# Gated linear attention with a cosine router: token rows made head by head on 64x64 tiles, in y's two PSUM banks, ahead of the scores and one chunk later

## The chip, the cores and the metric

The kernel runs on one core of one Trainium2 chip. The metric is the device time of one execution in microseconds; the time given for a kernel is the median of its runs. A profile is one execution recorded instruction by instruction. In it PE is TensorE's matrix multiply, PEld its weight load, DVE is VectorE, ACT is ScalarE, POOL is GpSimd and SP is SyncE, which issues most of the transfers.

## What is computed

Four batches of eight heads, 768 tokens each, head size 48, all in fp32. A gated linear attention gives `y`; its heads, side by side, are the 384 features of 3072 tokens. A router then picks one of eight experts for every token by the cosine between the token and an expert's embedding, and the expert is a two-layer network.

```python
for t in range(S):
    state = alpha[:, :, t, :, None] * state + np.einsum('bhd,bhe->bhde', k[:, :, t], v[:, :, t])
    y[:, :, t] = np.einsum('bhd,bhde->bhe', q[:, :, t], state)
...
x = y.transpose(0, 2, 1, 3).reshape(B * S, H * D)
xn = x / (np.linalg.norm(x, axis=-1, keepdims=True) + 1e-06)
en = expert_emb / (np.linalg.norm(expert_emb, axis=-1, keepdims=True) + 1e-06)
logits = xn @ en.T / tau
expert_idx = np.argmax(logits, axis=1)
...
for e in range(E):
    h = np.maximum(x[mask] @ w1[e], 0.0)
    out[mask] = gate_w[mask, None] * (h @ w2[e])
```

## The kernel before

The kernel has two phases. The first walks 24 chunks of 128 tokens (six for each batch) and makes the attention output; the second runs the eight experts over their tokens. The change touches only the first.

A head is padded from 48 to 64, so two heads fill 128 partitions. Four such pairs (`NP` = 4) make a chunk. `hh` is the head within a pair, 0 or 1, and it is also the half of the array's rows that the head's 64 features occupy.

The loop over `s` is a software pipeline written by hand. In step `s` TensorE does, in this order: `keys_back(s-1)` (decayed keys turned back, tile `pkb`); `decays(s)` (decay factors, keys and queries turned: tiles `pa`, `pk`, `pq`); `scores(s-1)` (key times query, tiles `sc0` and `sc1`); `mix_states(s-2)` and `mix_chunk(s-2)` (the state's and the chunk's own part of y, tiles `pyx0` and `pyx1`); `update(s-1)` (the new state, tile `pd`); and `rows(s-2)` (tile `px`). After a group of chunks that `GROUPS` names, `choose` (VectorE and GpSimd) picks each token's expert and `place` (TensorE tile `rk`, then VectorE) gives each token its row in the buffer `xs`, sorted by expert; `to_rows` sends the rows there with one indirect DMA per chunk from GpSimd. `in_turn()` pins the order of TensorE's instructions to the order of the calls; `behind(s)` puts small work behind the large VectorE and GpSimd operations of step `s`. The other engines' order is the scheduler's.

The PSUM memory has eight banks of 512 fp32 a partition, and the pools divide them: three for `ps_tr` (everything that is turned, and `px`), two for the scores, two for y (`ps_y`), one for `ps_mm`. A tile of a pool with one buffer is written anew in every step, and the framework inserts the waits: a writer waits for whoever still reads the tile's former content.

In `mix_chunk` the chunk's part of y is made in two halves. Four matmuls write `pyx0` from `sm0`, ScalarE copies `pyx0` to SBUF (`ycols0`, line 615), four matmuls write `pyx1` from `sm1`, and ScalarE copies `pyx1` (`ycols1`). The result is y with features on the partitions and tokens along the free dimension.

`rows` turns that into token rows, and makes the logits in the same pass: it multiplies y, as the stationary operand, by `sel`, which holds two 48-column identities and eight columns of scaled expert embeddings for each pair of heads. One matmul takes all 128 partitions (two heads), gives 64 tokens, and has 2 x 48 + 8 = 104 columns. ScalarE copies the logits (`lg`, line 637) and the rows (`x`, line 638) out of `px`, and VectorE adds up the logits (line 642).

At the end of the walk, steps 24 to 26, the last chunks are finished while the first layer of the first expert runs on the tokens that came early (`first_layer_early`, tile `phe`). The tokens of this early part are fetched by `fetch_early`, the first weights by `weights(0)`, both on SP's queue.

An fp32 matmul of the program stands in the profile as two records[...]; a transpose stands there as one.

Of the kernel before, what the change touches and what calls it, by code (L numbers as in the profile page):

```python
# [9 lines left out]
FP32 = mybir.dt.float32  # L10
# [17 lines left out]
def kernel(  # L28
# [26 lines left out]
    HALF = P // 2  # L55
# [3 lines left out]
    LG, TK, ROW = DM, DM + E, DM + E + 1  # L59
# [6 lines left out]
    S0, EARLY = 16, 2  # L66
# [123 lines left out]
    def mm(*args, **kwargs):  # L190
        last["pe"] = nc.tensor.matmul(*args, **kwargs)  # L191
# [4 lines left out]
    def in_turn():  # L196
        return tc.issue_after(last["pe"].ins) if last else ExitStack()


    with ExitStack() as c1:  # L200
# [40 lines left out]
        a_r, q_r, k_r, v_r = (t.rearrange(chunk_of, p=P) for t in (alpha, q, k, v))  # L241


        sel = keep.tile([P, 2, NP // 2, 2 * D + E], FP32, name="sel")
        group_of = [g for g, (a, b) in enumerate(GROUPS) for _ in range(a, b)]
        x_g = {}

# [5 lines left out]
        def prepare_fills():  # L253
            nc.gpsimd.memset(embp, 0.0)
            nc.gpsimd.memset(sel, 0.0)
            for hh in range(2):
                for q in range(NP // 2):
                    nc.gpsimd.tensor_copy(sel[0:DP, hh, q, 0:D], ident[0:DP, 0:D])
                    nc.gpsimd.tensor_copy(
                        sel[DP:P, hh, q, D : 2 * D], ident[DP:P, DP : DP + D]  # L260
                    )

        def prepare_loads():
            a0 = work.tile([NS, H, DP], FP32, name="a0", bufs=1)
# [36 lines left out]
        def turn_logits():  # L301

            pe = ps_tr.tile([P, 2, NP // 2, E], FP32, tag="tr", name="pe")
            for hh in range(2):
                for q in range(NP // 2):
                    tr(
                        pe[:, hh, q],
                        embp[:, hh, q].rearrange("e j d -> e (j d)"), ident[:E, :E],
                    )
            nc.vector.tensor_copy(sel[:, :, :, 2 * D :], pe)  # L310

        def to_rows(rows, x):
            ins = nc.gpsimd.indirect_dma_start(  # L313
# [269 lines left out]
        NQ = NP // 2  # L583
        YX = NQ * P

        def mix_states(s):
            d = st[s]
            d["pyx"] = pyx = [ps_y.tile([P, 512], FP32, name=f"pyx{hh}") for hh in range(2)]
            dec = d.get("dec")
            if dec is not None:  # L590
                for q in range(NQ):
                    for j in range(2):
                        for i in range(2):
                            hh, p = i, 2 * q + (i + j) % 2
# [22 lines left out]
        def rows(s):  # L617

            yT = st[s]["yT"]
            px = ps_tr.tile([P, 2, NQ, 2 * D + E], FP32, tag="tr", name="px")  # L620
            for hh in range(2):
                for q in range(NQ):

                    for i in range(2):
                        sl = slice(i * HALF, (i + 1) * HALF)
                        mm(
                            px[sl, hh, q], lhsT=yT[hh][:, q, sl], rhs=sel[:, hh, q],
                            start=True, stop=True, skip_group_check=True,
                        )
            g = group_of[s]  # L630
            s0, s1 = GROUPS[g]
            if s == s0:
                x_g[g] = work.tile([P, GMAX, ROW], FP32, name="x", bufs=4)[:, 0 : s1 - s0]
            x = x_g[g][:, s - s0]

            lg = work.tile([P, 2, NQ, E], FP32, name="lg", bufs=1)
            nc.scalar.copy(lg, px[:, :, :, 2 * D :])
            nc.scalar.copy(
                x[:, 0:DM].rearrange("t (q j a d) -> t a q j d", q=NQ, j=2, a=2),
                px[:, :, :, 0 : 2 * D].rearrange("t a q (j d) -> t a q j d", j=2),  # L640
            )
            nc.vector.tensor_reduce(
                x[:, LG : LG + E].unsqueeze(2), lg.rearrange("t a q e -> t e a q"),
                axis=AX.XY, op=ALU.add,
            )

# [28 lines left out]
        send = []  # L675
        placed_at = {}
        for g, (_, s1) in enumerate(GROUPS):
            soon = s1 == S0 or s1 > NS - 3
            placed_at.setdefault(s1 + (2 if soon else 3), []).append(g)
        warm(7)  # L680
        fixed_parts()
        load(0)
# [3 lines left out]
        for s in range(NS + 3):  # L686
            if s + 2 <= NS:
                v_last = load(s + 2)
            if s + 2 == NS:

                with tc.issue_after(v_last.ins):
                    weights(0)
            if 0 <= s - 1 < NS:
                with in_turn():
                    keys_back(s - 1)
            if s < NS:
                decays(s)
            if s == NS:
                with in_turn():
                    turn_early()  # L700
            if s < NS:
                decay_queries(s)
            if 0 <= s - 1 < NS:
                decay_state(s - 1)

                with in_turn(), tc.issue_after(st[s]["a_scan"].ins) if s < NS else ExitStack():
                    scores(s - 1)
            if s == 0:
                with behind(s), in_turn():
                    prepare_first(a0)  # L710
                with behind(s):
                    prepare_logits()
            if NS <= s < NS + 2:
                with in_turn():
                    first_layer_early(2 * (s - NS), 2 * (s - NS) + 1)
            if 0 <= s - 2 < NS:
                with in_turn():
                    mix_states(s - 2)
                with in_turn():
                    mix_chunk(s - 2)  # L720
            if 0 <= s - 1 < NS:

                with in_turn(), tc.issue_after(st[s]["a_scan"].ins) if s < NS else ExitStack():
                    update(s - 1)
            if 0 < s < NS and s % NCH == 0:

                with in_turn():
                    keys_back(s, ps_mm, "mm")
            if NS <= s < NS + 2:
                with in_turn():  # L730
                    first_layer_early(2 * (s - NS) + 1, 2 * (s - NS) + 2)
            if 0 <= s - 2 < NS:
                with in_turn():
                    rows(s - 2)
            if s == 1:
                with in_turn():
                    turn_logits()
            if s == 2:
                with behind(s):
                    routing_constants()  # L740
            if s == 3:
                with behind(s):
                    convert_constants()
            if 4 <= s < 4 + NXG * (NC + 1):
                i, t = divmod(s - 4, NC + 1)
                with behind(s):
                    nc.gpsimd.memset(xg_s[i][:, t], 0.0)
            if s == 3:
                with behind(s):
                    nc.gpsimd.memset(blank, 0.0)  # L750

            for g in placed_at.get(s, ()):
                r = GROUPS[g][1] - 1
                with in_turn():
                    n = place(g, r in (S0 - 1, NS - 1))
                if r == S0 - 1:
                    with behind(s):
                        first_expert(n)

            with behind(s) if s < NS else tc.issue_after(st[NS - 1]["masked"].ins):  # L760
                n_now = len(send) if s >= NS else 0 if s == NS - 1 else 1 + (len(send) > 2)
                for c in send[:n_now]:
                    to_rows(dest[:, c : c + 1], x_g[group_of[c]][:, c - GROUPS[group_of[c]][0]])
                    send.remove(c)
                    if c == S0 - 1:
                        fetch_early()
            if s == NS - 1:
                weights(1)
            r = s - 2
            if 0 <= r < NS:  # L770
                g = group_of[r]
                if r == GROUPS[g][1] - 1:
                    choose(g)
                    with behind(s) if s < NS else ExitStack():
                        nc.gpsimd.tensor_copy(x_g[g][:, :, TK], toks[:, slice(*GROUPS[g])])
            if s > NS:
                with in_turn():
                    first_layer_early(2 * (s - NS) + 2, 2 * (s - NS) + 4)
# [487 lines left out]
```

## Time and profile before

| | us |
|---|---|
| median of 3 runs | 416.75 |
| lowest and highest run | 415.18, 416.89 |
| the profiled execution, device time | 415.06 |
| span of that profile, first to last instruction | 413.3 |
| walk over the chunks, first to last `px` matmul | 18.8 to 150.2 |
| one step of that walk, where no routing falls in it | 5.6 |

The difference of 1.8 us between span and device time lies before the first and after the last instruction. The granted TensorE clock is 0.994 over the span. Busy time is given for each engine, and for TensorE it is modelled, since matmuls overlap: where one group of matmuls begins tells more than how long a single one lasts.

### The profile page before, as it was taken

The page shows a single profiled execution, that of the slowest core. Times are in us where ns is not written, and L with a number is a line of the kernel's source. Part 1 is how long each engine was busy: PE and PEld are TensorE (multiplying, and loading weights), DVE is VectorE, ACT ScalarE, POOL GpSimd, SP SyncE. Part 2 cuts the span into 40 slices and gives each one's busy share as a digit, 9 for nine tenths or more (in the row PEclk, how much of TensorE's full clock was granted, in tenths as well). Part 3 has the DMA queues.
Part 4 walks back from the last instruction along what each step waited for, and adds up shares of the span by engine and source line. Part 5 has one row for each costly group of instructions (what it writes and reads, how often), then busy time and mean ns, then how long its engine had stood idle before and what let it go on. Part 6 is the DMA issues. An engine that isn't in the chain of part 4 may idle for free. (4 is left out here: it accounts for less than half of the span.)

```text
span 413.3 us, 11425 instructions
## 1 busy us (share of the span) xinstructions
PE 403.6 (98%) x4346; PEld 358.6 (87%) x4346; DVE 267.8 (65%) x725; ACT 178.4 (43%) x430; POOL 190.9 (46%) x283
## 2 busy tenths in 40 slices
PE   6999999999999999999999999999999999999994
PEld 6888999899889886879799799799989979979974
DVE  6899788788898334715855845943672694593541
ACT  4555554555455435453523523522451352452410
POOL 7446787777766547308018028024301802702701
PEclk9999999999999999999999999999999999999999
DMA  9999999999998944959009219117303801001001
GB/s 137 160 162 157 159 214 172 199 182 205 194 185 257 387 172 143 293 186 365 6 18 321 92 39 329 56 38 272 121 19 105 302 2 38 22 0 53 3 17 43
DMA packets 119374, 60.20 MB, mean 146 GB/s; under 512 B 102287, under 2 KB 113816, under 8 KB 119312
## 3 DMA queue, kind: packets, MB, share of 16 engines
q1 hardware_dynamic: 115208, 49.14, 51.0%
q0 software_dynamic: 3728, 10.16, 7.1%
q8 instruction: 41, 0.67, 0.8%
q14 instruction: 21, 0.17, 0.1%
q10 hardware_dynamic: 376, 0.05, 0.1%
HBM read 49.69 MB, written 11.45 MB: 148 GB/s over the span
## 5 line engine op out<-in xcount | busy, mean ns | idle before, releaser
L817 POOL DMA_INDIRECT out_dram<-y,sx x25 | 24.4, 977 | 158.1 <-DVE gsh L873 77.6
L999 PE MATMUL pq<-xT,w 128*128 128x192 f32 x280 | 64.5, 328 | 0.6
L922 DVE TENSOR_TENSOR hT<-pq,v 128x192 f32<-128x192 f32 x84 | 30.0, 357 | 32.8 <-PE pq L999 30.8
L999 PEld LDWEIGHTS pq<-xT,w 128*128 128x128 f32 x280 | 47.3, 190 | 2.8 <-DVEq L1165 1.7
L507 POOL TENSOR_TENSOR qs<-qc,a 128x512 f32<-128x512 f32 x24 | 30.6, 1275 | 33.9 <-DVE a L503 23.4
L906 PE MATMUL pyo<-w,hT 128*128 128x384 f32 x128 | 43.3, 492 | 0.0
L906 PEld LDWEIGHTS pyo<-w,hT 128*128 128x128 f32 x128 | 23.7, 190 | 15.3
L999 PE MATMUL pq<-xT_m,w_m 128*128 128x192 f32 x168 | 36.5, 326 | 0.0
L1007 ACT ACTIVATE hT<-hT 128x384 f32<-128x384 f32 (+1 forms) x56 | 24.8, 443 | 23.1 <-DVE hT L922 19.9
L479 DVE TENSOR_TENSOR_SCAN r<-pa,inr 128x511 f32<-128x511 f32 x24 | 29.2, 1216 | 6.3 <-PE pa L194 4.4
L503 DVE TENSOR_TENSOR_SCAN a<-pa,ini 128x512 f32<-128x512 f32 x24 | 29.3, 1223 | 1.1
L1047 PE MATMUL pq<-w_m,hT_m 128*128 128x192 f32 x168 | 29.6, 326 | 0.0
L946 POOL TENSOR_TENSOR w_m<-w 128x384 f32<-128x384 f32 x28 | 27.4, 998 | 3.5 <-DMA out_dram<-y,sx 2.7
L999 PEld LDWEIGHTS pq<-xT_m,w_m 128*128 128x128 f32 x168 | 28.9, 190 | 0.0
L313 POOL DMA_INDIRECT xs<-x,dest x24 | 24.3, 1012 | 9.5 <-issue 4.5
L1007 ACT ACTIVATE hT<-pq 128x192 f32<-128x192 f32 x28 | 9.2, 330 | 43.5 <-PE pq L999 43.5
L1047 PEld LDWEIGHTS pq<-w_m,hT_m 128*128 128x128 f32 x168 | 27.7, 190 | 0.0
L946 POOL TENSOR_TENSOR w_m<-w,w_m 128x384 f32<-128x384 f32 x28 | 27.1, 996 | 0.0
L191 PE MATMUL sc<-qs,kr 64*64 64x128 f32 x768 | 26.5, 276 | 0.0
L191 PE MATMUL pyx<-sm,vt 128*64 128x128 f32 x384 | 26.3, 279 | 0.0
L922 DVE TENSOR_TENSOR v<-pq,v 128x192 f32<-128x192 f32 x56 | 20.0, 356 | 9.1 <-ACT v L1010 4.4
L1054 DVE SCALAR_TENSOR_TENSOR y<-pq,gt,u 128x192 f32<-128x192 f32 x21 | 8.8, 418 | 24.6 <-PE pq L1047 24.6
(199 smaller groups left out, 896.5 us busy)
## 6 DMA issues: line engine op xcount, KB each, us to landing
w<-in_moe_w_dram SPq DMA_DIRECT2D x16, 1536.0 KB, 9.2
kt<-in_k_dram SPq DMA_DIRECT2D x24, 192.0 KB, 4.3
qt<-in_q_dram SPq DMA_DIRECT2D x24, 192.0 KB, 4.5
vt<-in_v_dram SPq DMA_DIRECT2D x24, 192.0 KB, 5.8
xg<-xs SPq DMA_DIRECT2D x22, 196.5 KB, 7.7
at<-in_alpha_dram SPq DMA_DIRECT2D x24, 168.0 KB, 5.0
xg<-xs SPq DMA_DIRECT2D x8, 98.2 KB
at<-in_alpha_dram SPq DMA_DIRECT2D x24, 22.5 KB, 4.2
```

Source lines behind the costliest of these rows:

```text
L191: last["pe"] = nc.tensor.matmul(*args, **kwargs)
L313: ins = nc.gpsimd.indirect_dma_start(out=xs, out_offset=bass.IndirectOffsetOnAxis(ap=rows, axis=0), in_=x, in_offset=None, bounds_check=E ...
L479: nc.vector.tensor_tensor_scan(r[:, L - 2 :: -1], pa[:, L - 1 : 0 : -1], inr[:, L - 2 :: -1], 1.0, ALU.mult, ALU.add,)
L503: d["a_scan"] = by_dve = nc.vector.tensor_tensor_scan(a, pa, ini, 0.0, ALU.mult, ALU.add)
L507: by_pool = nc.gpsimd.tensor_tensor(qs.rearrange("p n t -> p (n t)"), d["qc"], a, ALU.mult)
L817: ins = nc.gpsimd.indirect_dma_start(out=out, out_offset=bass.IndirectOffsetOnAxis(ap=col, axis=0), in_=y, in_offset=None, bounds_check=N - 1,
L906: pe[:] = [nc.tensor.matmul(py, lhsT=hT[:, f], rhs=w2_t[:, f], start=(f == 0), stop=(f == FT - 1),)]
L922: dve[:] = [call(*args)]
L946: nc.gpsimd.tensor_tensor(to[:, f], x[:, f], y[:, f], ALU.subtract)
L999: pe[:] = [nc.tensor.matmul(to, lhsT=left, rhs=right, start=start, stop=stop, skip_group_check=True,)]
L1007: return nc.scalar.activation(h, p, AF.Relu)
L1047: pe[:] = [nc.tensor.matmul(to, lhsT=left[:, f], rhs=right[:, f], start=start and f == 0, stop=stop and f == n - 1, skip_group_check=True,)]
```

## The change

`rows` no longer takes two heads in one matmul. Each head has its own: 64 partitions of y, 64 tokens, and 48 + 8 = 56 columns, on one 64x64 quarter of the array. There are twice as many matmuls, 16 for a chunk in place of 8 (32 records in place of 16). The logits are then eight partial sums for a token instead of four, and ScalarE copies 64 numbers a token rather than 32.

The tile `px` is no longer in `ps_tr`. Both banks of y become one tile of two banks, `pyx`, which `y_banks()` hands out as two halves for `mix_states` and `mix_chunk`, and `rows` takes the same tile anew: heads in the lower half of the rows write its first bank, heads in the upper half its second.

`rows` moves. It stood at the end of the step, for chunk `s-2`; now it stands in front of `scores(s-1)`, for chunk `s-3`. In the last steps it is called twice to catch up: step 24 does chunk 21 in front and chunk 22 behind, step 25 does chunk 23. `choose` follows `rows`, so it comes one step later, and `placed_at` moves the groups: `place` comes a step later for all groups but the last two. The rows of chunks 16 to 19 are placed in step 24 rather than 23, and the sending of those rows follows it.

```diff
-        sel = keep.tile([P, 2, NP // 2, 2 * D + E], FP32, name="sel")
+        sel = keep.tile([P, 2, NP // 2, D + E], FP32, name="sel")
...
+        def y_banks():
+            both = ps_y.tile([P, 2, 512], FP32, name="pyx")
+            return both[:, 0], both[:, 1]
+
         def mix_states(s):
             d = st[s]
-            d["pyx"] = pyx = [ps_y.tile([P, 512], FP32, name=f"pyx{hh}") for hh in range(2)]
+            d["pyx"] = pyx = y_banks()
...
         def rows(s):
 
             yT = st[s]["yT"]
-            px = ps_tr.tile([P, 2, NQ, 2 * D + E], FP32, tag="tr", name="px")
+            both = ps_y.tile([P, 2, 512], FP32, name="pyx")
+            px = both[:, :, 0 : NP * (D + E)].rearrange(
+                "t j (a q c) -> t j a q c", a=2, q=NQ
+            )
             for hh in range(2):
                 for q in range(NQ):
-
                     for i in range(2):
-                        sl = slice(i * HALF, (i + 1) * HALF)
-                        mm(
-                            px[sl, hh, q], lhsT=yT[hh][:, q, sl], rhs=sel[:, hh, q],
-                            start=True, stop=True, skip_group_check=True,
-                        )
+                        to = slice(i * HALF, (i + 1) * HALF)
+                        for j in range(2):
+                            sl = slice(DP * j, DP * j + DP)
+                            mm(
+                                px[to, j, hh, q], lhsT=yT[hh][sl, q, to], rhs=sel[sl, hh, q],
+                                start=True, stop=True, skip_group_check=True,
+                            )
...
-            lg = work.tile([P, 2, NQ, E], FP32, name="lg", bufs=1)
-            nc.scalar.copy(lg, px[:, :, :, 2 * D :])
+            lg = work.tile([P, 2, NP, E], FP32, name="lg", bufs=1)
             nc.scalar.copy(
-                x[:, 0:DM].rearrange("t (q j a d) -> t a q j d", q=NQ, j=2, a=2),
-                px[:, :, :, 0 : 2 * D].rearrange("t a q (j d) -> t a q j d", j=2),
+                lg, both[:, :, 0 : NP * (D + E)].rearrange("t j (c e) -> t j c e", c=NP)[:, :, :, D:]
+            )
+            nc.scalar.copy(
+                x[:, 0:DM].rearrange("t (q j a d) -> t j a q d", q=NQ, j=2, a=2),
+                px[:, :, :, :, 0:D],
             )
...
-            soon = s1 == S0 or s1 > NS - 3
-            placed_at.setdefault(s1 + (2 if soon else 3), []).append(g)
+            late = 2 if s1 > NS - 3 else 3 if s1 == S0 else 4
+            placed_at.setdefault(s1 + late, []).append(g)
+
+        def rows_of(s):
+            if s < NS:
+                return [s - 3] if s >= 3 else []
+            return {NS: [NS - 3, NS - 2], NS + 1: [NS - 1]}.get(s, [])
...
             if s < NS:
                 decay_queries(s)
+            if 3 <= s <= NS:
+                with in_turn():
+                    rows(s - 3)
             if 0 <= s - 1 < NS:
                 decay_state(s - 1)
...
-            if 0 <= s - 2 < NS:
+            if NS <= s < NS + 2:
                 with in_turn():
                     rows(s - 2)
...
-            r = s - 2
-            if 0 <= r < NS:
+            for r in rows_of(s):
                 g = group_of[r]
                 if r == GROUPS[g][1] - 1:
                     choose(g)
```

More of the change, by code (lines that the diff above doesn't have):

```diff
@@ L258, in prepare_fills @@
                     nc.gpsimd.tensor_copy(sel[0:DP, hh, q, 0:D], ident[0:DP, 0:D])
-                    nc.gpsimd.tensor_copy(
-                        sel[DP:P, hh, q, D : 2 * D], ident[DP:P, DP : DP + D]
-                    )
+                    nc.gpsimd.tensor_copy(sel[DP:P, hh, q, 0:D], ident[DP:P, DP : DP + D])
         def prepare_loads():
@@ L309, in turn_logits @@
                     )
-            nc.vector.tensor_copy(sel[:, :, :, 2 * D :], pe)
+            nc.vector.tensor_copy(sel[:, :, :, D:], pe)
         def to_rows(rows, x):
@@ L624, in rows @@
                     for i in range(2):
-                        sl = slice(i * HALF, (i + 1) * HALF)
-                        mm(
-                            px[sl, hh, q], lhsT=yT[hh][:, q, sl], rhs=sel[:, hh, q],
-                            start=True, stop=True, skip_group_check=True,
-                        )
+                        to = slice(i * HALF, (i + 1) * HALF)
[5 more added lines that the diff above has]
+                            )
             g = group_of[s]
@@ L634, in rows @@
             x = x_g[g][:, s - s0]
-            lg = work.tile([P, 2, NQ, E], FP32, name="lg", bufs=1)
-            nc.scalar.copy(lg, px[:, :, :, 2 * D :])
+            lg = work.tile([P, 2, NP, E], FP32, name="lg", bufs=1)
             nc.scalar.copy(
-                x[:, 0:DM].rearrange("t (q j a d) -> t a q j d", q=NQ, j=2, a=2),
-                px[:, :, :, 0 : 2 * D].rearrange("t a q (j d) -> t a q j d", j=2),
+                lg, both[:, :, 0 : NP * (D + E)].rearrange("t j (c e) -> t j c e", c=NP)[:, :, :, D:]
[3 more added lines that the diff above has]
+                px[:, :, :, :, 0:D],
             )
             nc.vector.tensor_reduce(
-                x[:, LG : LG + E].unsqueeze(2), lg.rearrange("t a q e -> t e a q"),
+                x[:, LG : LG + E].unsqueeze(2), lg.rearrange("t j c e -> t e j c"),
                 axis=AX.XY, op=ALU.add,
```

## The prediction, made before the changed kernel ran

> **What bounds the kernel now.** I read the page's busy table first, then the busy time by stage, then the order of time within one step of the walk, then who waited for whom on TensorE.
>
> ```profile
> span 413.3 us, 11425 instructions
> PE 403.6 (98%) x4346; PEld 358.6 (87%) x4346; DVE 267.8 (65%) x725; ACT 178.4 (43%) x430; POOL 190.9 (46%) x283
> ```
>
> ```profile
> 58.22:63.82 5.60, 5.60 (x115) 5.09 (x113) 4.95 (x11) 3.07 (x7) 4.23 (x12) 1.00 1.21 205
> 63.82:69.41 5.59, 5.59 (x114) 5.08 (x113) 4.89 (x9) 3.07 (x7) 3.72 (x6) 1.00 0.84 148
> ```
>
> These are two whole steps (length, then PE, PEld, DVE, ACT, POOL busy, clock, DMA share, GB/s). PE has no gap in either, PEld is busy 91%, VectorE 88%, ScalarE only 55%. The next view, in order of time, shows why PE's figure can be believed here: its groups begin at a fixed pace.
>
> ```profile
> 60.14 1.10 PE L191 MATMUL sc<-qs,kr 64*64 64x128 f32 x32
> 60.30 0.59 ACT L489 COPY qc<-pq 128x512 f32<-128x512 f32 x1 [0.80 <-PE pq L194]
> ...
> 61.06 0.62 PE L191 MATMUL pyx<-qs,dec 64*64 64x128 f32 x16
> ...
> 61.61 1.09 PE L191 MATMUL pyx<-sm,vt 128*64 128x128 f32 x16
> ...
> 62.32 0.81 ACT L615 COPY ycols<-pyx 128x256 f32<-128x256 f32 x2 [0.34 <-PE pyx L191]
> ...
> 62.54 0.64 PE L191 MATMUL pd<-vt,kb 128*64 128x64 f32 x16
> ...
> 63.00 0.89 PE L191 MATMUL px<-sel,ycols 128*64 128x104 f32 x16
> ...
> 63.82 0.66 PE L194 MATMUL pkb<-ident,kr 128*128 128x128 f32 x4
> 63.93 0.18 ACT L637 COPY lg<-px 128x32 f32<-128x32 f32 x1 [0.81 <-PE px L191]
> ...
> 64.02 0.49 ACT L638 COPY x<-px 128x384 f32<-128x384 f32 x1
> ```
>
> Read the starts. 32 records of the scores take 0.92 us from start to start: eight sets of four (four quarters of the array at once), about 0.11 each for 128 columns. pyx<-sm: 16 records in 0.93, eight pairs, again 0.11 to 0.12. pd: eight pairs of 64 columns in 0.46, 0.058 each. px: 0.82. So the walk is bound by TensorE's stream, and what is added to or taken from TensorE there counts in full. The waits of TensorE's weight loads between 10 and 150 us confirm it: ACT's copy of y holds it three times in all.
>
> ```profile
> PEld px L191 <- issue: 0.7, 2, 0.3
> PEld pkb L194 <- issue: 0.5, 3, 0.2
> ...
> PEld px L191 <- ACT ycols L615: 0.5, 3, 0.2
> ```
>
> **What the Trainium skill says.** "TensorEngine Tiling (Array Packing)", Key Properties: changing the tiling mode drains TensorE. The trace agrees: pq to sc takes 0.55 where pk to pq took 0.44, and dec to sm 0.55 where four sets of 0.11 make 0.44, so a switch costs 0.11. "PSUM — Partial Sum Buffer", on collisions: row tiles may not write one bank at the same time, hence two banks for the two heads; nothing in this trace tests that. "TensorE: Matmul & The Clock Gate", on the measured gaps, has a floor of about 25 ns from one matmul's start to the next. The trace's smallest sustained spacing is 0.46/16 = 29 ns, so it cannot settle whether four quarters share that floor. "Perfetto Trace Analysis", Identifying Dependency Chains, advises reading an instruction's own list of semaphores. I did that for the changed program, and it decides this forecast.
>
> **The change part by part**, against the profiled execution's 415.06 us (span 413.3 and 1.8 around it; the median of the runs, 416.75, is 1.7 higher).
>
> 1. The matmuls of rows. Removed: px's 0.82 less one switch of 0.11 = 0.71, eight pairs of 0.089. The switch stays, it now falls between pd and pkb: three switches a step before (pq to sc, dec to sm, px to pkb) and three after. Added: 32 records of 56 columns in eight sets of four. The nearest row is pd, 64 columns on the same 64-wide weight load, at 0.058; by columns alone (0.109 for 128, 0.089 for 104) it would be 0.051. I take 0.055: 0.44. Gain 0.27 a chunk, times 24 = 6.6. Bounds: 0.30 a chunk (7.2), and below nothing: with the skill's floor shared by the quarters 32 x 0.025 = 0.80, a loss of 2.2 in all.
>
> 2. A wait inside y. Before, pyx0 and pyx1 were two tiles; now both banks are one tile. In the changed program the first matmul of the second half (sm1 into the second bank) has, beside its wait for GpSimd's mask, a new wait on ScalarE, and its value is the copy ycols0 of the same chunk. It is there in all 24 chunks. The first half must thus be finished, copied out by ScalarE and signalled before TensorE may write the second bank. From the lines above: the first half starts at 61.61, the second at about 61.61 + 0.49 = 62.10 (half of the 0.93, with the switch at its front); the first copy starts at 62.32 and lasts 0.372 (each of the 48 copies does, in the view of the tile ycols), so it ends at 62.69. Then comes a signal of about 0.05 (px ended at 63.89, lg began at 63.93) and a restart with its weights not loaded ahead, which I price at 0.05 as half a switch. 62.79 less 62.10 = 0.70 a chunk, times 24 = 16.8. Bounds 0.60 and 0.80 (14.4 to 19.2). Behind the waiting matmul stand the rest of the half, pd, and the next step's pkb and pa: everything on TensorE. VectorE gets pa later, but it is 88% busy of a step that gets longer, so nothing else is late because of it.
>
> 3. A wait in front of y. mix_states writes the tile that ScalarE reads for lg and x; the changed program lists that wait on x, at the first dec matmul. Say the rows' matmuls start at 0. Their last starts at 0.50 and ends 0.22 later (pd's mean record, 0.222), 0.72; ScalarE has finished qc at 0.17 + 0.59 = 0.76; lg begins there, and x ends 0.66 to 0.69 after px's end as in the lines above (63.89 to 64.51), so at about 1.43, and is seen at 1.48. The scores cover it until 0.49 + 0.92 = 1.41. Left over: 0.07, and with the restart 0.12, times the 21 chunks with this sequence = 2.5. Bounds 0 and 5 (0.24 each): the cover is the scores alone, and it is short by a hair.
>
> 4. What goes away: the two switches more that pkb's late place brought at the three batch ends where it stood between y and px, 3 x 0.22 = 0.7; and place's wait for GpSimd's sums at 109.2, 0.5 (the group of chunks 14 and 15 now has nearly a whole step between choose and place). 1.2 together, 0.6 to 1.5.
>
> 5. The last steps. The rows of chunks 16 to 19 are now placed in step 24 behind px(22), and the changed program puts their four indirect DMAs on GpSimd in front of the sums that place needs in step 25. With px(22) at 0: dest is there at 1.65, four DMAs of 1.29 (start to start) run from 1.9 to 7.0, three sums 0.25 each to about 7.6. TensorE reaches that rk at 6.3 without part 2 and 7.0 with it: 0.6 of waiting. Bounds 0 and 1.5. Behind it stand twelve phe matmuls and the second layer.
>
> 6. At nothing: ScalarE's 32 more numbers for lg (about 0.03 of the 45% it is idle); the reduction likewise on VectorE; choose's five operations now in front of sm0 on VectorE, about 1.2 late, but the scores' banks are needed only about 2.4 later. SP's loads and the early fetch move by one step at most, and since TensorE gets slower they have more room: the early tokens landed near 128 and are turned at 137.6.
>
> Sum: -6.6 + 16.8 + 2.5 - 1.2 + 0.6 = +12.1. On the profiled execution that is 427.2, on the median 428.8.
>
> **The rivals.**
>
> *The wait inside y does not bite* (the other side: faster). One mechanism: the second bank's first matmul finds the copy done, or ScalarE's read is short enough to lie under work already queued. Its place is the step from sm0 to sm1, its price part 2's 16.8, and it turns to a gain once this wait costs less than 0.20 a chunk (4.7 / 24). For it: the two halves are in different banks and no data passes between them. Against: the wait is in the program, TensorE runs in order, and the copy ended 0.59 after the second half began. Time: 416.75 - 6.6 + 2.5 - 1.2 + 0.6 = 412.1. Chance 0.08.
>
> *The quarters do not run four at once for short matmuls.* Each set of four costs four issue slots, so rows takes 0.80 or more, and everything else is as forecast: 6.6 + 2.2 more, 437.6. For it: 25 ns is a floor on the skill's page, and no row here goes below 29. Against: the scores' sets of four begin in one burst. Chance 0.12.
>
> *Gain and waits cancel* (within 2 us): the wait is half as long and the restart free, about 417. Chance 0.03.
>
> **How the numbers follow.** The forecast has 0.77. Its own range, from the bounds of parts 1 to 5 taken not all at once, is 423 to 434. With 0.12 at 437.6 and 0.11 below, 422 to 437 leaves out the faster cases and the upper part of the second rival, about 0.2. About 0.5%, 2 us, is what a measurement of this kernel tells from no change. Faster 0.08, same 0.03, slower 0.89.
>
> **What would show it.** Right: in the list of waits a row of some 24 waits of PEld pyx on ACT ycols, about 0.6 each; a second, smaller one on ACT x; the step 6.1 to 6.2 instead of 5.59; rows in 0.40 to 0.48 from its start to the scores' start; PE busy with gaps in the walk. Wrong: no such waits (first rival), or rows at 0.8 (second). If the walk is longer but by less, the restart was cheaper than part 2 has it. The experts' phase should keep its length.

## The result, and the profile after

The changed kernel took 438.88 us (median of 4 runs, 437.70 to 440.45) against 416.78 us before (415.18 to 416.89): ratio 1.054, 95% interval 1.050 to 1.058. It is slower, as forecast, but by 22.1 us and not by 12.0, and it lies above the range that was given. The profiled execution has 438.62 us and a span of 436.8, 23.5 more than the span before.

The head of the page and one whole step of the walk by window (length, then PE, PEld, DVE, ACT, POOL busy with instruction counts, clock, DMA share, GB/s):

```profile
span 436.8 us, 12224 instructions
PE 403.5 (92%) x4730; PEld 352.5 (81%) x4730; DVE 273.8 (63%) x725; ACT 179.1 (41%) x430; POOL 190.9 (44%) x283
```

```profile
59.10:65.32 6.22, 5.66 (x141) 4.89 (x136) 4.40 (x7) 3.09 (x8) 4.98 (x7) 1.00 1.09 233
```

PE's busy time is what it was (403.6 before). The span grew, so what came in is idle time: PE filled a whole step before, and now it stands for 0.56 us of it (and again in the step after this one). The view in order of time says where (start, length, engine, line, operation, and in brackets the idle time ahead of it and what ended it):

```profile
64.86 0.69 PE L191 MATMUL pyx<-sel,ycols 64*64 64x56 f32 x32
...
65.37 1.06 PE L191 MATMUL sc<-qs,kr 64*64 64x128 f32 x32
...
65.73 0.49 ACT L646 COPY x<-pyx 128x384 f32<-128x384 f32 x1
...
66.27 0.67 PE L191 MATMUL pyx<-qs,dec 64*64 64x128 f32 x16
...
66.87 0.66 PE L191 MATMUL pyx<-sm,vt 128*64 128x128 f32 x8
...
67.57 0.37 ACT L617 COPY ycols<-pyx 128x256 f32<-128x256 f32 x1 [0.41 <-PE pyx L191]
...
68.09 0.66 PE L191 MATMUL pyx<-sm,vt 128*64 128x128 f32 x8 [0.56 <-ACT ycols L617]
...
68.55 0.66 PE L191 MATMUL pd<-vt,kb 128*64 128x64 f32 x16
...
69.14 0.66 PE L194 MATMUL pkb<-ident,kr 128*128 128x128 f32 x4
```

Read the starts on PE. rows to scores 0.51; scores to dec 0.90 (0.92 before); dec to the first half 0.60 (0.55); first half to pd 1.68 (0.93), of which first half to second half is 1.22; pd to pkb 0.59, where pd, px and the switch took 1.28. So a step gains 1.28 - 0.59 - 0.51 = 0.18 by the new matmuls, loses 0.75 inside y and 0.03 around dec: +0.60, and the step went from 5.59 to 6.20.

24 times 0.60 are 14.4 us of 23.5. Most of the other 9 stands in the list of PE's waits (total us, times, longest). Its first row is the wait inside y; the row counts PE's idle time alone, 0.56 each, while by the starts, which don't depend on the modelled ends, it costs 0.75 a chunk.

```profile
PE pyx L191 <- ACT ycols L617: 13.5, 24, 0.6
PE pq L1015 <- issue: 2.1, 2, 1.7
PE rk L191 <- DVE state L555: 1.9, 2, 1.3
...
PE rk L191 <- ACT kb L522: 1.3, 2, 0.7
PE sc L191 <- issue: 0.9, 1, 0.9
...
PE rk L191 <- DVE state L553: 0.5, 1, 0.5
```

Two things are new here. rk, the small matmul of place, waits five times, 3.7 us in all, where before only one wait of 0.5 stood. And PE stands three times, 3.0 us in all, in the middle of a row of like matmuls for nothing that the profile shows ("issue"): once in the scores of step 24, twice in the experts' phase. Last, the end: from the issue of the last scatter to the end of the span it is 6.27 us (430.58 to 436.85) against 4.08 (409.19 to 413.27), 2.2 more.

The longest of rk's waits, in order of time:

```profile
105.63 0.66 PE L191 MATMUL pd<-vt,kb 128*64 128x64 f32 x16
...
106.40 0.17 DVE L337 TENSOR_TENSOR chosen<-win,best 128x16 f32<-128x16 f32 x1
106.50 0.68 DVE L572 TENSOR_TENSOR sm<-sc,causal 128x512 f32<-128x512 f32 x1
...
107.10 0.41 DVE L555 TENSOR_TENSOR state<-pd,dec 128x256 f32<-128x256 f32 x1
...
107.56 0.41 PE L191 MATMUL rk<-before,ones 128*128 128x32 f32 x2 [1.27 <-DVE state L555]
```

rk and pd are allocated in the same single bank (ps_mm). Before, px stood between them, and in its 0.82 us VectorE had read pd:

```profile
101.51 0.64 PE L191 MATMUL pd<-vt,kb 128*64 128x64 f32 x16
...
101.97 0.89 PE L191 MATMUL px<-sel,ycols 128*64 128x104 f32 x16
102.26 0.42 DVE L557 TENSOR_TENSOR state<-pd,dec 128x256 f32<-128x256 f32 x1
...
102.79 0.40 PE L191 MATMUL rk<-before,ones 128*128 128x16 f32 x2
```

Now rk is next to pd; and choose, one chunk later, has come to stand on VectorE directly in front of the mask sm0 and of state, which reads pd. (In the view after, `chosen` is the last operation of choose.) The two waits on kb are the same at batch ends, where the early pkb has the bank.

### The profile page after: what moved, and what is told of

The parts are those of the page before. It is cut to its first block, busy times and chain, and to the rows that moved or that the text cites. A ratio compares the mean times of both kernels' runs of the same rounds, so it can differ in the third digit from the quotient of the medians.

```text
span 436.8 us, 12224 instructions
## 1 busy us (share of the span) xinstructions
PE 403.5 (92%) x4730; PEld 352.5 (81%) x4730; DVE 273.8 (63%) x725; ACT 179.1 (41%) x430; POOL 190.9 (44%) x283
## 5 line engine op out<-in xcount | busy, mean ns | idle before, releaser
L191 PE MATMUL pyx<-sm,vt 128*64 128x128 f32 x384 | 31.6, 283 | 13.5 <-ACT ycols L617 13.5
L191 PEld LDWEIGHTS pyx<-sm,vt 128*64 128x64 f32 x384 | 20.7, 136 | 22.8 <-issue 22.2
L617 ACT COPY ycols<-pyx 128x256 f32<-128x256 f32 x48 | 17.9, 372 | 28.9 <-PE pyx L191 28.8
```

## The experiments

All figures are medians; a ratio is to the kernel before on the same chip. place_only, form_only, behind_and_rk and behind_and_choose ran on a chip on which the kernel before took 424.66 us; of these only the ratios are compared with the others. The kernel before has no trace on that chip. The four traces taken there all hold a wait of 2.0 us on xT in the second phase that no other trace has, so their lists of waits are not compared entry by entry with the others.

### The wait inside y: taken away in two ways, and put into the kernel before

y_copies_behind, on the changed kernel:

```diff
@@ mix_chunk @@
                     mm(pyx[hh][...], lhsT=vt[:, 2 * p + hh], rhs=sm[hh][:, p], ...)
-                nc.scalar.copy(yT[hh].rearrange("p q t -> p (q t)"), pyx[hh][:, 0:YX])
+            for hh in range(2):
+                nc.scalar.copy(yT[hh].rearrange("p q t -> p (q t)"), pyx[hh][:, 0:YX])
```

> The changed kernel with one edit: in mix_chunk both halves of the matmuls (sm0, sm1) come first and the two ScalarE copies after them, so that the second half no longer waits for the copy of the first. Theory (the wait inside y costs 0.73 us a chunk, 24 times): 438.9 - 17.3 = 421.5 us (419 to 424), sm0 start to sm1 start back from 1.22 to about 0.5, step about 5.5 us; still slower than before, because waits of place's rk for its bank (about 5 us) and stalls of TensorE that the trace calls issue (about 3 us in the profiled execution) stay. Rival (the waits behind it move up: sm1 then waits for GpSimd's mask, or VectorE becomes the bound): gain of under 8 us, 431 or more.

Measured: 424.04 us, ratio 1.020 (1.014 to 1.025), 14.9 us less than the changed kernel. A step is 5.41 us, 0.18 under the one before the change. That is 2.5 us short of the forecast, and the list of PE's waits shows where most of it lies:

```profile
PE rk L191 <- DVE state L555: 3.2, 2, 2.4
...
PE rk L191 <- DVE state L553: 1.5, 1, 1.5
PE rk L191 <- ACT kb L522: 1.4, 2, 0.7
PE rk L191 <- POOL before L340: 1.2, 1, 1.2
```

With PE faster, VectorE is later against it: rk's waits rise from 4.2 to 7.3 us, the one at GpSimd's sums included. They take back about 3 of the 24 x 0.75 = 18.0 that the wait inside y cost.

y_two_tiles, on the changed kernel:

```diff
 def y_banks():
-    both = ps_y.tile([P, 2, 512], FP32, name="pyx")
-    return both[:, 0], both[:, 1]
+    return [ps_y.tile([P, 512], FP32, name=f"pyx{j}") for j in range(2)]
...
-            nc.scalar.copy(lg, both[...])
-            nc.scalar.copy(x[...], px[:, :, :, :, 0:D])
+            for j in range(2):
+                nc.scalar.copy(lg[:, j], both[j][...])
+            for j in range(2):
+                nc.scalar.copy(xr[:, j], px[j][:, :, :, 0:D])
```

> The changed kernel with pyx taken as two tiles of one bank each (as before), for y and for rows; rows' copies to lg and x become one per bank, so ScalarE has two small copies more in a chunk. The wait inside y goes in another way, the order of copies stays. Theory: the same 421.5 us (419 to 424.5) as with the copies behind; the second bank's dec matmul has a little more time for its x copy. Rival (it is not the shared tile, but the ScalarE copy sits between the halves for another reason, e.g. the order in which the instructions are put on TensorE): no gain, about 438.

Measured: 425.91 us, ratio 1.022 (1.018 to 1.025), a little above the 419 to 424.5 expected (the trace has 4.0 us of "issue" on PE). The wait goes here too, with the order of the copies as it was. So it came from the two banks being one tile, and from nothing in the data.

before_one_y_tile, on the kernel before:

```diff
-            d["pyx"] = pyx = [ps_y.tile([P, 512], FP32, name=f"pyx{hh}") for hh in range(2)]
+            both = ps_y.tile([P, 2, 512], FP32, name="pyx")
+            d["pyx"] = pyx = both[:, 0], both[:, 1]
```

> The kernel before with one edit: pyx as one tile of two banks; rows as they were, in ps_tr and one chunk earlier. Theory (the wait inside y alone): 416.8 + 24 x 0.70 = 433.6 us (431 to 436). Rival (the wait costs this only together with rows' new place): under 427.

Measured: 434.42 us, ratio 1.043 (1.040 to 1.046): 17.7 us from these lines alone, with rows untouched. Part 2 of the forecast had 16.8.

### rk's bank and choose

rk_other_bank, on the changed kernel:

```diff
-            bank = ps_mm.tile([P, GMAX + 1, E], FP32, tag="mm", name="rk")
+            bank = ps_tr.tile([P, GMAX + 1, E], FP32, tag="tr", name="rk")
```

> The changed kernel with place's bank rk taken from the pool of three banks (ps_tr) and no longer from the single bank that pd and the early pkb use. Theory (rk stands right behind pd now and waits for VectorE's state or ScalarE's kb to free the one bank, 2.1 + 1.8 + 0.7 us in the list of waits of the changed kernel): 438.9 - 4.5 = 434.4 us (433 to 436.5). Rival (the wait only moves: pa, pk or rows then wait for the three banks, or VectorE is late anyway): 438 to 440.

Measured: 434.21 us, ratio 1.042 (1.039 to 1.045), 4.7 us less than the changed kernel. One wait of 1.4 us turned up at pq, on at_row, which reads rk.

behind_and_rk has this edit and that of y_copies_behind.

> The changed kernel with both edits: copies of y behind both halves, and rk in the pool of three banks. Theory (with the wait inside y gone, rk's waits for the one bank are 7.3 us in the trace of the copies-behind kernel, of which 5 to 6 go and the rest turns up at pq or pa): 424.0 - 5.5 = 418.5 us (417 to 421). Rival (VectorE is late in those steps whatever bank rk has, so that the scores' masks or kr wait instead): 423 or more.

Measured: ratio 1.014 (1.010 to 1.019), against 1.020 with the copies alone: 2.2 us, not 5.5; the two intervals leave about 3 us either way, so the 2.2 are not clear of the noise. Waits of 2.2 and 0.7 us of pq and pk on at_row took the place of part of rk's: VectorE reaches at_row late, because choose stands in front of it. This is the rival's reading, with pq and pk late instead of the masks.

behind_and_choose leaves rk in its bank and moves choose:

```diff
-                    choose(g)
+                    with tc.issue_after(carried["by"].ins) if s < NS else ExitStack():
+                        choose(g)
```

(`carried["by"]` is the last state operation of update.)

> The changed kernel with the copies of y behind both halves, and choose's five VectorE operations issued behind state of the same step instead of in front of sm0 and state. rk stays in the single bank. Theory (rk waits there because choose stands in front of state on VectorE): the waits of 0.8, 2.4 and 1.5 us at rk shrink to under 0.6 each, 424.0 - 3.5 = 420.5 us (419 to 422). Rival (state is late by its own work, choose does not matter): 424.

Measured: ratio 1.011 (1.008 to 1.015): (1.0197 - 1.0114) x 417 = 3.5 us less than with the copies alone, as expected, again with about 3 us either way. In the traces rk's waits fall from 7.3 to 4.0 us; one of 0.8 and the one on the first state of a batch (1.3) stayed. So the order on VectorE is one cause of rk's waits. Whether the order or the bank weighs more, these two runs do not tell.

### The place alone and the form alone

place_only is the kernel before with rows called a chunk later in front of the scores (the last three hunks of the change), px still in ps_tr:

> The kernel before with rows only moved (a chunk later, in front of the scores, batches placed as in the changed kernel); its matmuls, its tile in ps_tr and y's two tiles are as before. Theory: 416.8 + rk's waits for the one bank (about 6) + one more mode switch in a step (pq, px, sc: 0.11 x 21 = 2.3) - 1.2 + 0.6 = 424.5 us (421 to 427), rk's waits on state in the list; no stalls of TensorE called issue within one kind of matmul, because it has the 4346 records of before. Rival (the place costs nothing, all of the rest lies in the form of the matmuls): under 419.

Measured: ratio 1.066 (1.062 to 1.069), some 27 us. Neither theory had this.

```profile
PE px L191 <- DVE kr L486: 17.8, 16, 1.3
PE px L191 <- DVE ini L499: 5.5, 4, 1.5
```

px is now the fourth tile (after pa, pk and pq) that wants one of three banks in quick succession, and it waits for VectorE to work through r and kr. At the old place those reads were long done. So rows can't move to the new place at no cost while px stays in ps_tr.

The same trace says where rk's waits come from: it has five of them on state and kb, 3.4 us in all, with the old matmuls and y's two tiles untouched. In form_only, next, with the new matmuls at the old place, one of 0.3 is left. They come with the place.

form_only is the converse: 64x64 tiles in y's two banks (two tiles, split copies) at the old place.

> The changed form only: rows on 64x64 tiles in y's two banks (as two tiles, split copies), but at the old place and chunk of the kernel before. Theory: 416.8 - 24 x (0.71 - 0.44 - 0.11 for the switch that comes back) = 413.0 us by the matmuls, plus some 3 us of stalls called issue at the program places where the changed kernel has them (4730 records): 416 us (413 to 419); no waits of rk for its bank beyond the 0.5 of before. Rival (these stalls come from the place and not from the number of records): 413 or less. Rival (the form costs more than it gives): over 420.

Measured: ratio 1.011 (1.008 to 1.014), 4.7 us more and not 1 less, on the side of the second rival. pd to pkb by the starts of the weight loads is 0.67 + 0.69 = 1.36 where the kernel before has 1.39: a gain of 0.03 instead of 0.18. The switch that comes back takes 0.1, and the rows themselves take 0.08 more than at the new place (0.69 less 0.1, against 0.51). On top of it PE waited 1.9 us for kb at pq, 1.2 for ycols, 1.1 for GpSimd, and 4 us for "issue". How much of these waits belongs to this chip is open.

### The three edits together, and 64x128 tiles

fixed_three has the copies behind, choose behind state and rk in ps_tr.

> The changed kernel with all three edits: copies of y behind both halves, choose behind state, rk in the pool of three banks. Theory: rk's waits (3.5 us in the trace with the first two edits) go, waits of pq or pk on at_row stay under 1 us; ratio to before from 1.011 to 1.003 (1.000 to 1.007). Rival (the waits only move to pq and pk): 1.010 or more.

Measured: 418.17 us against 416.70, ratio 1.0046 (1.0026 to 1.0066). Three edits that touch none of the new matmuls take back 20.7 of the 22.1 us. What is left shows in PE's waits:

```profile
PE pq L194 <- DVE at_row L362: 2.2, 1, 2.2
...
PE rk L191 <- POOL before L340: 1.2, 1, 1.2
```

The row left out is an "issue" stall of 2.1 us in the scores. The wait on at_row was expected under 1 us; it is one place, at choose of chunks 14 and 15, where VectorE's running sum waits 0.86 us for GpSimd's and at_row stands behind it.

fixed_three_wide has rows on 64x128 tiles as well, half the records:

```diff
-                    for i in range(2):
-                        to = slice(i * HALF, (i + 1) * HALF)
-                        for j in range(2):
-                            sl = slice(DP * j, DP * j + DP)
-                            mm(px[to, j, hh, q], lhsT=yT[hh][sl, q, to], rhs=sel[sl, hh, q], ...)
+                    for j in range(2):
+                        sl = slice(DP * j, DP * j + DP)
+                        mm(px[:, j, hh, q], lhsT=yT[hh][sl, q], rhs=sel[sl, hh, q], ...)
```

> As with the three edits, and rows' matmuls on 64x128 tiles (all 128 tokens at once): again eight sets in a chunk, but two matmuls in a set instead of four, so 4346 records. Theory: one more mode switch a step (0.11 x 24 = 2.6 us more) against no stalls called issue (3 us less) and the same time for the sets: equal to the three edits alone within 2 us, and no stall of over 0.3 us within one kind of matmul. Rival (the stalls stay with half the records): 2 to 3 us slower than the three edits alone. Rival (short sets are cheaper with two matmuls than with four): rows 0.3 instead of 0.46 a chunk, 3 us faster.

Measured: 427.17 us, ratio 1.024 (1.020 to 1.028), 9 us slower than fixed_three. All three forecasts of the time missed: rows to scores, by the starts of the weight loads, is 1.03 us instead of 0.46.

The two 64-row tiles did run at the same time. Taken record by record, rows' matmuls start in pairs 0.007 us apart: at 0, 0.153, 0.265, 0.377 us and so on, 0.112 from pair to pair. Their weight loads come in pairs 0.11 apart too. What has changed is that a load now has 128 columns instead of 64. rk in the kernel before shows the same pace with nothing tiled: its loads have 128 columns, its matmuls stream only 8 to 32, and they start 0.11 apart. pd's loads of 64 columns go with pairs 0.058 apart. So where a set streams fewer columns than its weights have, it lasts as long as the weight load: 8 x 0.112, 0.04 more for the first pair and the switch of 0.1 make the 1.03.

No "issue" stall is left, but there are fewer and longer records, so this doesn't tell which of them counts.

form_old_place, the 64x128 tiles in y's two banks at the old place:

> rows on 64x128 tiles in y's two banks (two tiles, split copies), at the old place and chunk of the kernel before: 4346 records. Theory: pd to pkb 1.24 us a step instead of 1.39, as with 64x64 tiles at the old place (0.67 + 0.69 = 1.36 there with one switch more) or a little less, no stalls called issue: ratio to before 0.99 to 1.00. Rival (ScalarE's split copies and the wait on ycols give it back): 1.005 to 1.012.

Measured: 424.29 us, ratio 1.019 (1.017 to 1.020). The same cause again, in the view in order of time:

```profile
65.29 0.64 PE L191 MATMUL pd<-vt,kb 128*64 128x64 f32 x16
65.85 1.17 PE L191 MATMUL pyx<-sel,ycols 64*128 64x56 f32 x16
66.95 0.66 PE L194 MATMUL pkb<-ident,kr 128*128 128x128 f32 x4
```

pd to rows is 0.56 (0.46 for pd itself, 0.10 for the switch) and rows to pkb 1.10: 1.66 in place of 1.28, or 9 us in 24 chunks, somewhat more than the 7.6 measured. The two tiles' records do not start together here (0, 0.077, 0.154, 0.231, 0.265 us), but each tile's go on at 0.112 again.

### The number of records, and the stalls again

before_split, on the kernel before: each of px's matmuls in two of 52 columns.

```diff
-                        mm(px[sl, hh, q], lhsT=yT[hh][:, q, sl], rhs=sel[:, hh, q], ...)
+                        for c in (slice(0, D + E // 2), slice(D + E // 2, 2 * D + E)):
+                            mm(px[sl, hh, q, c], lhsT=yT[hh][:, q, sl], rhs=sel[:, hh, q, c], ...)
```

> The kernel before with each of rows' matmuls cut into two of 52 columns: the same work on the same tiles at the same place, but 4730 records of TensorE like the changed kernel, instead of 4346. Theory (the stalls called issue in the changed kernel are TensorE waiting for its own instructions, and come with their number): stalls of 1 to 2 us within one kind of matmul after 120 us, together 2 to 5 us; px itself 0 to 0.1 us longer a chunk; so 3 to 6 us above before. Rival (the stalls belong to the changed order or to chance): no such stall, within 2 us of before.

Measured: 424.13 us, ratio 1.019 (1.016 to 1.023), and no "issue" stall after 120 us in spite of 4730 records. So their number alone does not make the stalls; that theory fell. The 7.4 us have another cause, seen in the order of time (px to pkb; before, these lines had 63.00 and 63.82):

```profile
65.82 1.14 PE L191 MATMUL px<-sel,ycols 128*64 128x52 f32 x32
66.90 0.66 PE L194 MATMUL pkb<-ident,kr 128*128 128x128 f32 x4
```

px to pkb is 1.08 where it was 0.82, 6.2 us in 24 chunks; the end after the last scatter is 1.1 longer. Taken record by record, the pairs of 52 columns follow each other at 0.058 us, as pd's pairs of 64 do, where a pair of 104 takes 0.089. Half the columns are not half the time: with loads of 64 weight columns there is a floor of 0.058 a set. The new rows' sets of four stand on it too: they start at 0, 0.100, 0.158, 0.217, 0.275 us, 0.058 apart but for the first, which takes 0.04 more.

after_again is the changed kernel, profiled a second time.

> The changed kernel once more, for a second trace. Theory (stalls belong to the program: same records wait for the same instructions): a stall of about 0.9 us in the scores of step 24, one of 1.5 to 2 us near the start of the second expert, 0.4 near the end; the tail after the last scatter is chance, 4 or 6 us. Rival (all of it chance): the stalls are elsewhere or gone, and the trace is 2 to 3 us shorter for it.

Measured: 439.22 us, ratio 1.054 (1.051 to 1.058).

```profile
PE pq L1015 <- issue: 2.2, 2, 1.7
...
PE sc L191 <- issue: 0.6, 1, 0.6
```

The stalls are back, at the same three records of PE in both traces (numbers 2838, 3463 and 4585): 0.63, 1.68 and 0.50 us here, 0.91, 1.68 and 0.42 there. The end after the last scatter is long again (5.86). So both belong to the program and are no accident of one execution. In both traces a packet of 16 KB of instructions was fetched by DMA at each of the stalls; it landed 1.3 to 1.6 us before PE went on. Such packets come all along the program (44 in the trace of the changed kernel, 41 in that of the kernel before, which has no such stall), so that one is near says little; but in all twelve traces of kernels with rows on 64x64 tiles, every stall of more than 0.43 us ends 1.2 to 1.7 us after one has landed. That PE waited for its instructions is the likely reading; no run shows it apart, nor why most packets cost nothing.

### A version that keeps the new matmuls

best_order has the three edits and two more: choose is also issued behind place's last VectorE operation of the step, and the running sums of the last four chunks are VectorE's.

```diff
-                eng = nc.vector if s in (S0 - 1, NS - 1) else nc.gpsimd
+                eng = nc.vector if s == S0 - 1 or s >= NS - 4 else nc.gpsimd
...
-                        choose(g)
+                        with tc.issue_after(carried["dest"].ins) if "dest" in carried else ExitStack():
+                            choose(g)
```

> The three edits, choose also behind place's last VectorE operation in the same step, and the running sums of the last four chunks on VectorE instead of GpSimd. Theory: pq's wait on at_row (2.2 us) and rk's on GpSimd (1.2 us) go: 418.2 - 3.2 = 415.0 us (413.5 to 416.5), slightly faster than before. Rival (choose, later still, makes sm0 or kr late instead): 417 or more.

Measured: 414.39 us (22 runs), ratio 0.9957 (0.9943 to 0.9970): faster than before by 1.8 us by the ratio (2.4 by the medians), and by 24 than the changed kernel. A step, by window, has no gap any more:

```profile
59.37:64.78 5.41, 5.41 (x141) 4.88 (x136) 4.88 (x11) 3.00 (x8) 4.41 (x9) 1.00 0.93 194
```

The wait on at_row is gone; a wait of rk on GpSimd of 1.2 us has moved to the batch of chunks 14 and 15. 24 x 0.18 = 4.3 us is what the form gives at its new place in the walk; 1.0 us of "issue" in step 24 and an end of 6.0 us (1.9 more than before) take most of the difference to the measured gain. The kernel before was not given the two last edits, so how much of the gain they would have brought alone is open; that the step is 0.18 shorter is read from the trace.

best_order_qc moves ScalarE's copy qc behind lg and x:

> As best_order, and ScalarE's copy qc behind rows' copies lg and x instead of in front of them, so that x is out 0.1 to 0.2 us earlier. Theory: the scores to dec take 0.82 instead of 0.95 us, 0.08 to 0.13 a step: 2 to 3 us less than best_order, 412.5 us. Rival (qc late makes qs or sm1 late, and the scores wait): not faster than best_order, or slower.

Measured: 415.05 us, ratio 0.9971 (0.9956 to 0.9986): no gain. In both kernels' order of time lg begins 0.76 us after rows' start, with qc in front of it or not. The last of rows' results, not ScalarE, sets it.

best_order_turn puts the rows of chunk 21 ahead of the transposes in step 24:

> As best_order_qc, with the rows of chunk 21 in front of the early tokens' transposes in step 24, so that 32 records of rows and 32 of scores do not follow each other there. Theory (the stall of 1 to 2 us in that step's scores is TensorE running out of instructions after a burst of short records): no stall there, 1 to 2 us less than best_order_qc. Rival (the stall comes at a given place of the program whatever stands there): the same time within 1 us, the stall shown at the same record number.

Measured: 414.93 us, ratio 0.9955 (0.9938 to 0.9971), as best_order. The stall is there again (1.8 us), at record 2845, the same as in best_order_qc. The burst of short records is not its cause; the rival stands.

## Why the forecast was right in direction and short by ten microseconds

By its own parts, from the two traces (us over the whole walk):

| part | forecast | found | from |
|---|---|---|---|
| 1, matmuls of rows | -6.6 | -4.3 | 24 x 0.18 |
| 2, wait inside y | +16.8 | +18.0 | 24 x 0.75; alone +17.7 in before_one_y_tile |
| 3, dec on x | +2.5 | +0.6 | 21 x 0.03 |
| 4, rk's wait goes | -0.5 | +3.2 | 3.7 new less 0.5 old |
| 5, rk on GpSimd in step 25 | +0.6 | +0.5 | one wait |
| not forecast: stalls "issue" | 0 | +3.0 | three |
| not forecast: end after the last scatter | 0 | +2.2 | 6.27 - 4.08 |
| sum | +12.8 | +23.2 | span: +23.5 |

(The forecast's two mode switches at each of three batch ends, 0.7 less, were not measured apart.)

**Right.** The direction, the cause and its size: the second half of y waits for the copy of the first in all 24 chunks, because two banks had become one tile. Three runs show it from both sides (y_copies_behind, y_two_tiles, before_one_y_tile). It was short by 0.05 a chunk: from the end of the copy to PE's next start it is 0.15 (67.94 to 68.09), where 0.10 was taken. Part 5 was right as well: the four DMAs and then the three sums stand in front of rk, which waits 0.5.

**The step that failed is part 6, and with it part 4.** The forecast moved choose in front of sm0 on VectorE and costed it at nothing, because "the scores' banks are needed only about 2.4 later". It asked for the wrong follower. Behind sm0 on VectorE stands state; state frees the one bank of ps_mm; and the next to need that bank is rk, 0.6 us after pd, since px no longer stands between. Part 4 counted only the 0.5 that rk would no longer wait for GpSimd; that wait did go, and five others came. The runs show 3.7 us of waits on that bank (4.7 us in rk_other_bank), that they come with the move of rows (3.4 us in place_only, 0.3 in form_only), and that choose is one cause (3.5 us in behind_and_choose). The forecast listed what the moved operation waits for and did not list what the removed px had been hiding.

This step is 3.7 of the 10.4 us between the two sums. Another 5.2 are the two rows that the forecast did not have, and 2.3 are part 1; parts 2, 3 and 5 nearly cancel.

**Part 1 was mis-sized.** It took 0.055 us for a set of 56 columns, between pd's 0.058 and a figure by columns of 0.051 (its own two points, 0.109 and 0.089, give 0.049). The sets took 0.058, the same as pd's with 64, and the first 0.04 more, 0.51 in all instead of 0.44: a set doesn't get shorter than the load of its 64 weight columns. The gain is 0.18 a chunk, not 0.27. The rival in which the quarters share issue slots and take 0.80 a chunk did not happen (0.51). The trace of before already spoke against it: the four records of the first set of scores start within 21 ns (at 0, 7, 15 and 21), and dec's 16 records in 0.44 us are 27 ns each, below the 29 that was called the smallest.

**Part 3** was right in its order: dec begins 0.05 us after x's end in 18 of 20 steps. But the scores cover that wait: scores to dec is 0.90, no longer than before (0.92), and only the 0.05 that dec to the first half takes longer, less that 0.02, is left.

**"The experts' phase should keep its length"** was wrong by 4.3 us: two stalls of 2.1 together and the longer end. Nothing in the diff touches that phase. A forecast from the trace of before had no row for it; the range had no room for it either, and without these 4.3 us the median would have lain inside it.

## What to carry to other kernels

Before two tiles are made one, look for a reader of one half that stands between the writers of both: the wait goes by tile and not by bank, and here it cost 0.75 us a chunk, four times the gain. When an operation is taken out from between two others, ask which wait its time had hidden, and whose buffer is next in line, in particular in a pool of one. Short matmuls that each need new weights are not priced by the columns they stream: here a set took 0.058 us with 52, 56 or 64 streamed columns on 64 weight columns, and 0.11 with 8 to 56 streamed columns on 128. Measure the short form before counting columns.

## What the runs showed that was not expected

- 64x64 tiles ran four at a time (32 records in 0.51 us) and 128x64 tiles two at a time (pd, 16 records in 0.46), and two 64x128 tiles also two at a time, but at half the pace (16 records in 0.92 us): their weight loads are twice as wide.
- On 64 weight columns a pair of 52 streamed columns takes 0.058 us, one of 64 takes 0.058, one of 104 takes 0.089.
- Stalls of over 0.4 us (up to 2.1) with nothing that PE waits for in the profile occur in all twelve traces here of a kernel with rows on 64x64 tiles, and in none of the six without. The two traces of the changed kernel have them at the same records, and in eleven of the twelve one falls in the scores of step 23 or 24. The number of records is not enough for them (before_split has two of 0.3 us and no longer one), and short records before the stall are not needed (best_order_turn). What sets them stays open.
- The end after the last scatter is 4.1 us in the kernel before and in before_one_y_tile, 4.5 in place_only and 5.1 to 6.4 in the others. In the trace of the changed kernel a 16 KB packet of instructions is under way while the last pieces of the scatter land, and in the kernel before it begins only after them; but in form_only it also begins after them and the end is 5.6. The cause stays open.
